# A new order of the work for a polysketch attention and MetaFormer kernel, with epsilon added on GpSimd

## The chip, the core and the metric

The kernel runs on one core of one Trainium2 chip. A core has TensorE (matrix multiply, PE in the profile), VectorE (DVE), ScalarE (ACT), GpSimd (POOL) and SyncE (SP, which here only issues transfers). The metric is device time in microseconds; what is compared is the median of several runs.

## What is computed

Inputs are q, k, v of shape (4 batches, 4 heads, 1088 rows, 32), two sketch matrices S1, S2 of 8 x 32, a scale g of 128 and two MLP matrices of 128 x 512 and 512 x 128. The weights arrive in 64-bit floats. The reference, cut to what matters:

```python
def phi(x):                      # 8 x 8 = 64 features of a row
    a = np.einsum('rd,bhsd->bhsr', S1, x)
    b = np.einsum('rd,bhsd->bhsr', S2, x)
    return np.einsum('bhsi,bhsj->bhsij', a, b).reshape(*x.shape[:-1], r * r)
q_p, k_p = phi(q), phi(k)
kv = np.einsum('bhsf,bhsd->bhfd', k_p, v)
z = np.sum(k_p, axis=2)
num = np.einsum('bhsf,bhfd->bhsd', q_p, kv)
den = np.einsum('bhsf,bhf->bhs', q_p, z)[..., None] + 1e-06
x = (num / den)                  # then (B, H, S, D) -> (B, S, 128)
xn = (x - mean(x)) / np.sqrt(var(x) + 1e-06) * g
out = x + np.maximum(xn @ w_ch1, 0.0) @ w_ch2
```

## The kernel before

All work is a flat list of small named operations, the string `PROGRAM` (L824 to L909), written out in the source; a loop at L910 calls them one after the other. Each operation issues one or a few instructions to one engine, so the string fixes the order on every engine: every engine runs its own instructions strictly in the order of the list and waits at an instruction until what it reads is ready and what it overwrites is free. The tile framework (`manual_schedule`, L65) only puts in the semaphores. SyncE's transfers are also issued in the order of the list, and a transfer that must wait holds up those behind it. The first argument of many operations says the engine (V VectorE, A ScalarE, G GpSimd, S SyncE); numbers behind it are batch or chunk, a range of row groups, and the banks of PSUM (`ALL`, eight banks of 512 columns).

Each batch of 1088 rows is two chunks of 512 rows and 64 rows left over. Chunks 0 to 7 belong two by two to batches 0 to 3; chunks 8 and 9 collect the 64-row rests of two batches each. Row groups u of 128 rows are counted 0 to 8: 0 to 4 is the first chunk of a batch, 4 to 9 the second with the rest.

What a batch goes through:

- Loads: `ld` (k, and q of batches 1 to 3), `ld_t` and `ld_tr` (q of batch 0, by heads and halves), `ld_v` and `ld_vr` (v by groups), all on SyncE's queue. `ld_s` (S1, S2) is on ScalarE's queue, `ld_g` on GpSimd's, `ld_w` brings the two halves of w1 (256 KB each) and w2 (512 KB).
- Weights: `w_ex`, `w_bits`, `w_exf`, `w_mant`, `w_low`, `w_e2`, `w_e3`, `w_add` or `w_addlow`, and `w_mul` turn the words of the 64-bit floats into 32-bit floats (index 0: S, 1: w1, 2: w2). `s_heads` writes S for all heads (tile `s_f`); `sk`, `sk_0`, `sk_8`, `sk_2`, `sk_d` spread it into the forms that the matmuls read. `fold` and `fold_cp` multiply the centring and g into w1.
- k features: `turn_g`, `turn_r` transpose k on VectorE (L414, L424); batch 0 multiplies with `k_dir` (L448) and copies with `k_cp`, the others use `k_feat` (L466) and `k_tok` (L475). `k_prod0` and `k_prod` make the 64 products (tile `kp`, one buffer), `k_sum`, `k_zs`, `k_sc`, `k_sccp` the sum z, `k_val` (L519) the product with v, `k_vcp`, `k_spr`, `k_rcp` bring it into the form `kvr`.
- q features: batch 0 turns q on TensorE (`turn_p`, `turn_c`) and uses `q_dir` (L554) and `q_cp`; the others use `q_feat` (L587) and `q_tok` (L596). `q_ac`, `q_den`, `q_rec` make 1/den, `q_a2` scales by it, `q_prod` makes the 64 products, `q_turn` (L634) transposes them.
- `num` (L648) is the numerator, 32 matmuls of 32 x 32 tiles for one range of rows. `num_cp` and `num_r` copy it, transposed, to `xT`, from which the MLP reads. `row_turn` (L710) makes rows of it, `row_wr` and `row_rd` pass them through DRAM.
- MLP: `hid` (L757) is one quarter of the hidden layer of a chunk (512 columns at most), `relu` (L765, L767) empties it, `sec` (L773) is the second matrix for 128 rows. The normalisation's scale comes from `st_bn`, `st_ag` and `st_pow` (statistics, variance plus epsilon, power -0.5: tiles `st`, `mv`, `va`, `rstd`) and is put on afterwards by `fin`, or by `fin_a` and `fin_g`, which also add x. `store` and `store_r` write the output.
- `fill` (L247) multiplies ones at the start, with no use of the result.

In the list before, batch 0 does its numerators in the order `num 0 0 4`, `num 0 4 9`, and the MLP begins with chunk 0 in eight half-wide `hid` of 256 columns. `st_ag` adds epsilon on VectorE (L737), `st_pow` raises to the power on GpSimd (L743).

Of the kernel before, what the change touches and what calls it, by code (L numbers as in the profile page):

```python
# [25 lines left out]
def kernel(  # L26
# [705 lines left out]
    @op  # L732
    def st_ag(c):
        n, st, mv = tiles(c), sts[slot(c)], mvs[slot(c)]
        for t in range(n):
# [1 line left out]
        dve.tensor_tensor(out=vas[slot(c)][:, 0:n], in0=_ap(mv, 0, P, 1, [[2, n]]),  # L737
                          in1=eps[:, 0:n], op=ALU.add)
# [116 lines left out]
    row_turn 1 1 2 3; w_low A 2 0 512; hid 5 0 3 2 4; q_den 1 4 9; ld_v S 1 0; hid 3 0 0 2 4;
    ld_vr S 1 1; w_exf V 2 0 512; ld_v S 2 0; turn_g k 3 0 4; turn_r k 3; relu A 0 0 1 0 2;
    ld_v S 2 2; ld_vr S 2 1; relu A 4 1 3 0 4; row_turn 1 0 6 7; q_a2 G 1 0 4; num_r A 0 6 7;
    q_prod G 1 0 4; hid 0 0 1 2 4; hid 4 0 2 2 4; relu A 0 0 1 2 4; row_wr S 1; q_rec 1 4 9;
    k_feat 3 6 7; turn_r q 2; relu A 1 0 3 0 2; ld_v S 3 2; hid 0 1 2 0 4; ld_v S 2 3;
    row_wr S 0; q_a2 G 1 4 9; q_prod G 1 4 9; w_e2 G 2 0 512; turn_g q 2 0 4; relu A 4 0 2 2 4;  # L860
# [83 lines left out]
```

## Time and profile before

| what | value |
|---|---|
| median of 3 runs | 113.13 us (111.95 to 113.26) |
| span of the profiled execution, first to last instruction | 111.1 us; the page gives no other time of this execution |
| busy: TensorE, VectorE, ScalarE, GpSimd | 98.5, 82.4, 36.7, 52.9 us |
| mean granted clock of TensorE | 0.965 |
| HBM read, written | 9.84 MB, 4.33 MB |

The profile is one execution recorded by the hardware. Its page gives the busy time of each engine, the span in 40 slices (each digit the busy share in tenths, 9 for 90% and more; the clock row the clock that was granted), the transfers, the chain of work that ended last, and the costliest groups of instructions by line. Other views of the same trace are a timeline (start, length, engine, line, operation, output<-input, count, and in brackets the idle time before with what ended it), the list of waits (who waited for whom, total, times, longest), and a table of stretches. PEld is TensorE's loading of weights, which overlaps its matmuls; a 32-bit matmul appears as two weight loads and two matmuls. L87 and L82 are helper lines for products and copies, so there the tile names tell what is meant. What ends a wait is inferred from semaphores, and "issue" means that the profile shows nothing that was waited for.

### The profile page before, as it was taken

How to read it: one execution, taken by the hardware profiler on the slowest of the kernel's cores; microseconds unless marked ns; L12 is line 12 of the kernel's file. 1: busy time of each engine (PE TensorE's matmuls, PEld its weight loads, DVE VectorE, ACT ScalarE, POOL GpSimd, SP SyncE). 2: the span in 40 equal slices, each digit the busy share in tenths (PEclk: the TensorE clock that was granted, in tenths of full speed). 3: DMA queues.
4: the chain of work that ended last, by engine and by line, in shares of the span. 5: the costliest groups of instructions: out<-in, count | busy, mean ns of one | idle time of the engine just before them, and what ended most of it. 6: DMA issues, size and time to landing. Idle time of an engine off the chain costs nothing.

```text
span 111.1 us, 3153 instructions
## 1 busy us (share of the span) xinstructions
PE 98.5 (89%) x1271; PEld 69.7 (63%) x1271; DVE 82.4 (74%) x238; ACT 36.7 (33%) x91; POOL 52.9 (48%) x70
## 2 busy tenths in 40 slices
PE   4988997891499999999999997999999999999960
...
PEclk9999999999556999999999999999999999999998
...
GB/s 31 262 249 249 285 249 204 279 252 246 91 6 120 163 122 298 40 94 112 83 102 51 0 0 100 44 110 139 113 171 6 101 289 59 50 0 187 12 135 74
DMA packets 16992, 14.37 MB, mean 129 GB/s; under 512 B 6609, under 2 KB 13777, under 8 KB 16977
## 3 DMA queue, kind: packets, MB, share of 16 engines
...
q8 instruction: 10, 0.16, 0.7%
q10 hardware_dynamic: 112, 0.04, 0.1%
...
q0 software_dynamic: 32, 0.00, 0.0%
HBM read 9.84 MB, written 4.33 MB: 127 GB/s over the span
## 4 chain that ended last, share of the span: by engine, by line
PE 65%; DVE 18%; DMA 9%; SPq 3%; issue 2%; DVEq 0%
PE ALL L757 27%; PE ALL L773 25%; DMA kn<-in_k_dram 9%; PE ALL L648 6%; PE ALL L519 4%; DVE qpT L634 3%; DVE kT L414 2%; SPq L143 2%; DVE hT L767 2%; DVE va L737 2%; DVE bits L279 2%; DVE fq L596 1%; DVE kf L475 1%; PE ALL L504 1%; DVE st L730 1%
## 5 line engine op out<-in xcount | busy, mean ns | idle before, releaser
L773 PEld LDWEIGHTS ALL<-w,hT 128*128 128x128 f32 x272 | 32.2, 192 | 3.9 <-issue 2.3
L773 PE MATMUL ALL<-w,hT 128*128 128x128 f32 x272 | 33.3, 277 | 0.0
L757 PE MATMUL ALL<-xT,w 128*128 128x512 f32 (+1 forms) x72 | 32.4, 586 | 0.0
L765 ACT ACTIVATE hT<-ALL 128x512 f32<-128x512 f32 (+2 forms) x31 | 14.0, 493 | 23.5 <-PE ALL L757 22.6
L743 POOL TENSOR_TENSOR rstd<-va,mhalf 128x4 f32<-128x4 f32 (+1 forms) x10 | 9.2, 926 | 23.8 <-DVE va L737 15.1
L757 PEld LDWEIGHTS ALL<-xT,w 128*128 128x128 f32 x72 | 13.8, 210 | 9.5 <-issue 5.3
L87 POOL TENSOR_TENSOR kp<-kf 128x1280 f32<-128x1280 f32 (+2 forms) x7 | 14.4, 2069 | 0.0
L87 POOL TENSOR_TENSOR qp<-a,fq 128x512 f32<-128x512 f32 (+3 forms) x8 | 13.3, 1678 | 0.8 <-DVE a L87 0.6
L648 PE MATMUL ALL<-qpT,kvr 32*32 32x288 f32 (+2 forms) x320 | 8.1, 388 | 4.2 <-DVE rden L616 3.9
L634 DVE STREAM_TRANSPOSE qpT<-qp 128x1280 f32<-128x1280 f32 (+2 forms) x9 | 11.1, 1230 | 0.0
L791 ACT ACTIVATE ob<-ALL,rstd 128x128 f32<-128x128 f32 x20 | 6.3, 368 | 14.3 <-PE ALL L773 9.4
L767 DVE TENSOR_SCALAR hT<-ALL 128x512 f32<-128x512 f32 (+1 forms) x13 | 7.5, 589 | 4.5 <-PE ALL L757 4.4
L82 ACT COPY xT<-ALL 128x256 f32<-128x256 f32 x12 | 7.0, 658 | 9.8 <-PE ALL L648 9.8
L648 PEld LDWEIGHTS ALL<-qpT,kvr 32*32 32x32 f32 x320 | 4.6, 108 | 8.0 <-issue 3.6
L710 DVE STREAM_TRANSPOSE xh<-ALL 128x256 f32<-128x256 f32 x16 | 6.6, 426 | 2.8 <-ACT xT L82 1.8
L730 DVE BATCH_NORM_STATS2 st<-x 128x6 f32<-128x128 f32 x32 | 6.7, 270 | 2.2 <-DMA x<-xd 2.2
L247 PE MATMUL ALL<-ones 128*128 128x512 f32 (+1 forms) x14 | 6.9, 635 | 1.4 <-DVE ones L190 1.4
L414 DVE STREAM_TRANSPOSE kT<-kn 128x1024 f32<-128x1024 f32 (+1 forms) x5 | 5.1, 1022 | 1.8 <-DMA kn<-in_k_dram 1.8
L305 POOL TENSOR_SCALAR ex<-exf 128x256 uint32<-128x256 f32 (+1 forms) x2 | 3.1, 1535 | 7.0 <-DVE exf L287 6.9
L519 PEld LDWEIGHTS ALL<-kp,vn 128*32 128x32 f32 x288 | 4.3, 110 | 2.7 <-issue 2.3
L786 DVE SCALAR_TENSOR_TENSOR ob<-ALL,rstd,x 128x128 f32<-128x128 f32 x12 | 4.0, 346 | 2.6 <-PE ALL L773 2.6
L519 PE MATMUL ALL<-kp,vn 128*32 128x64 f32 x288 | 5.1, 220 | 0.9 <-issue 0.9
...
## 6 DMA issues: line engine op xcount, KB each, us to landing
vn<-in_v_dram SPq DMA_DIRECT2D x16, 128.0 KB, 5.3
...
```

The source lines that it names most:

```text
L82: act.copy(o, i)
L87: by[eng].tensor_tensor(out=o, in0=a, in1=b, op=ALU.mult)
L414: dve.transpose(_ap(dst[b % 2], 0, P, 32 * g0, [[32, g1 - g0], [P, 8], [1, 32]]), src[b][:, 256 * g0 : 256 * g1],)
L519: pe.matmul(bank(z, 0, F)[D * h : D * h + D], vn[b][:, TW * h + D * u : TW * h + D * (u + 1)], kp[:, H * F * u + F * h : H * F * u + F * ( ...
L634: dve.transpose(_ap(qpT, 0, P, 32 * u0, [[32, u1 - u0], [TW, 8], [1, 32]]), qp[:, H * F * u0 : H * F * u1])
L648: pe.matmul(bank(z[r], o, o + w)[D * h : D * h + D], kvr[b % 2][rows, DM * f + D * h : DM * f + D * h + D], qpT[rows, c : c + w], start=(f ...
L730: dve.bn_stats(out=sts[slot(c)][:, 6 * t : 6 * t + 6], in_=row_ap(c, t))
L743: pool.tensor_tensor(out=rstds[slot(c)][:, 0:n], in0=vas[slot(c)][:, 0:n], in1=mhalf[:, 0:n], op=ALU.pow)
L757: pe.matmul(bank(z, 0, n), w1[:, P * j : P * (j + 1)], cols(c)[:, a : a + n], start=True, stop=True)
L765: act.activation(o, i, AF.Relu)
L767: by[eng].tensor_scalar(out=o, in0=i, scalar1=0.0, scalar2=None, op0=ALU.max)
L773: pe.matmul(bank(z, DM * t, DM * (t + 1)), h[:, 512 * j + P * t : 512 * j + P * (t + 1)], w2[:, DM * j : DM * (j + 1)], start=(j == 0), st ...
```

## The change

`st_ag` no longer adds epsilon; `st_pow` adds it on GpSimd before the power. All else is the list: the same 522 operations, each once, in another order, some of them on another engine (of w2's conversion, `w_e2` and `w_exf` leave GpSimd and VectorE for VectorE and ScalarE, `w_mul` goes from VectorE to GpSimd) and with other PSUM banks. In batch 0 the second range of rows goes first: `q_dir`, `q_prod`, `q_turn` and `num` for 4 to 9 stand ahead of those for 0 to 4, and the MLP begins with chunk 1 in four `hid` of 512 columns; `num 0 0 4` follows behind these. The transfers have a new order too: one half of w1 and one of k 0 first, w2 and v 0 ahead of k 2 and q 1. Of the list, the start and the part around `num 2` to `num 3` are shown, old and then new.

```diff
@@ -734,12 +734,12 @@
         n, st, mv = tiles(c), sts[slot(c)], mvs[slot(c)]
         for t in range(n):
             dve.bn_aggr(out=mv[:, 2 * t : 2 * t + 2], in_=st[:, 6 * t : 6 * t + 6])
-        dve.tensor_tensor(out=vas[slot(c)][:, 0:n], in0=_ap(mv, 0, P, 1, [[2, n]]),
-                          in1=eps[:, 0:n], op=ALU.add)
 
     @op
     def st_pow(c):
         n = tiles(c)
+        pool.tensor_tensor(out=vas[slot(c)][:, 0:n], in0=_ap(mvs[slot(c)], 0, P, 1, [[2, n]]),
+                           in1=eps[:, 0:n], op=ALU.add)
         pool.tensor_tensor(out=rstds[slot(c)][:, 0:n], in0=vas[slot(c)][:, 0:n],
                            in1=mhalf[:, 0:n], op=ALU.pow)
 
@@ -822,90 +822,89 @@
@@ -822,90 +822,89 @@
     PROGRAM = """
-    c_iota; c_ones; ld_t S 0 4 8; ld_s A 1; ld_t S 0 0 4; ld_s A 0; fill 1 512 7; w_ex V 0 0 64;
-    w_exf V 0 0 64; c_pads 1; c_masks; fill 1 256 6; ld_w S 1 0 2; fill 1 512 7; w_low A 1 0 256;
-    w_bits V 1 0 256; ld S k 0 16 34; c_ident; c_small; c_vpad 0; w_bits V 0 0 64;
-    w_ex V 1 0 256; w_mant V 0 0 64; ld_t S 1 4 8; ld_t S 1 0 4; w_e2 V 0 0 64; ld S k 0 0 16;
-    ld_w S 1 2 4; fill 1 512 6; turn_r k 0; w_e3 V 0 0 64; ld_tr S; w_exf A 1 0 256; c_vpad 3;
-    w_addlow V 0 0 64; s_heads V; ld_t S 2 4 8; turn_g k 0 0 2; w_mant A 1 0 256; c_ac 0; sk 7;
-    fill 1 512 6; sk_0 7; ld_t S 2 0 4; fill 1 256 5; turn_g k 0 2 4; k_dir 0 0 3 6; sk_2 7;
-    c_pads 0; ld S k 1 0 34; w_ex V 1 256 512; ld_t S 3 0 4; k_dir 0 6 9 5; w_add V 1 0 256;
-    k_dir 0 3 6 4; w_bits V 1 256 512; sk_8 7; w_exf V 1 256 512; w_mant V 1 256 512; c_vpad 2;
-    ld_t S 3 4 8; k_cp A 0 0 3 6; sk_q 7; ld S k 2 0 34; ld_g; turn_p 3 8 9; w_e2 V 1 0 256;
-    w_low A 1 256 512; fill 1 256 2; k_cp A 0 6 9 5; ld_v S 0 1; k_cp A 0 3 6 4; sk_d 7;
-    w_e3 V 1 0 256; k_sum 0 5; turn_p 2 0 4; turn_c A 2 0 4; w_e2 G 1 256 512; ld_v S 0 0;
-    k_prod0 0 3 6 0; w_add V 1 256 512; turn_r k 1; w_e3 V 1 256 512; ld S q 1 0 34; ld_vr S 0 0;
-    ld_v S 0 2; ld_v S 0 3; k_zs 0 5; k_sc 0 5; k_prod0 3 6 4 3; turn_p 6 4 8; k_sccp A 0 5;
-    turn_g k 1 0 4; q_dir 0 4 2; ld_vr S 0 1; turn_c A 3 8 9; turn_g k 2 0 4; turn_c A 6 4 8;
-    w_mul G 1 256 512; q_dir 4 9 6; k_prod G 0 6 9; q_cp A 0 4 2 0 24; q_ac G 0 0 4;
-    k_feat 1 2 3; q_cp A 4 9 6 0 24; w_mul G 1 0 256; q_den 0 0 4; c_cg G; turn_r k 2;
-    q_rec 0 0 4; q_ac V 0 4 9; c_ac 1; q_a2 V 0 0 4; q_den 0 4 9; k_tok 1 2 3; q_rec 0 4 9;
-    fold 4 0 256; q_prod G 0 2 4; c_rest; q_a2 V 0 4 9; k_feat 2 5 6; k_tok 2 5 6;
-    q_prod G 0 0 2; q_prod G 0 6 9; k_sum 1 7; q_prod G 0 4 6; turn_r q 1; sk_qq 2; k_sum 2 3;
-    k_zs 1 7; turn_g q 1 0 4; k_sc 1 7; fold 6 256 512; fold_cp A 6 256 512; k_sccp V 1 7;
-    q_turn 0 2; k_zs 2 3; k_val 0 0 3 5; q_turn 2 4; k_val 0 3 6 5; c_vpad 1; k_val 0 6 9 5;
-    k_sc 2 3; ld_v S 1 2; ld_v S 1 3; k_vcp A 0 5; ld_w S 2 0 4; k_spr 0 5; k_rcp A 0 5;
-    k_sccp V 2 3; ld S k 3 0 34; ld_vr S 1 0; q_turn 4 9; q_feat 1 6 7 2 3; q_tok 1 0 6 7;
-    q_tok 1 1 2 3; ld_v S 3 3; fold_cp A 4 0 256; w_bits V 2 0 512; num 0 0 4 0 1 4 5;
-    num_cp A 0 0 0 4 0 1; num_cp A 0 1 0 4 4 5; num 0 4 9 6 7 2 3; k_prod G 1 0 5; q_ac V 1 4 9;
-    q_ac V 1 0 4; row_turn 0 0 0 1; hid 0 0 0 0 2; ld_v S 2 1; w_ex V 2 0 512;
...
-    fin_a 6 2 3; fin_g V 0; q_feat 3 0 1 6 7; q_tok 3 0 0 1; q_tok 3 1 6 7; fin_a 2 1 2;
-    k_prod G 3 0 5; q_ac G 3 4 9; fin_a 3 2 0; num 2 0 9 2 3 4 5; num_cp A 2 0 0 4 2 3;
-    store S 0 0 4; k_val 3 0 9 0; num_cp A 2 0 4 8 2 3; q_ac G 3 0 4; row_turn 5 1 4 5;
-    num_cp V 2 1 4 8 4 5; row_turn 4 1 4 5; hid 7 8 3 0 1; relu A 7 8 3 0 1; k_vcp V 3 0;
...
+    ld_w S 1 2 4; ld_s A 0; c_pads 1; c_small; c_ones; ld_g; c_act; ld S k 0 0 16; ld_s A 1;
+    fill 1 256 1; ld_w S 1 0 2; c_ac 0; c_vpad 1; c_vpad 0; ld_tr S; c_iota; c_ident;
+    fill 1 256 3; c_masks; ld_t S 3 4 8; c_vpad 3; fill 1 512 7; c_pads 0; ld S k 0 16 34; c_rest;
+    w_ex V 1 256 512; w_ex V 0 0 64; w_exf V 1 256 512; ld_t S 1 4 8; w_e2 V 1 256 512;
+    w_bits V 1 256 512; ld_t S 0 4 8; w_bits V 0 0 64; fill 1 512 2; w_exf V 0 0 64;
+    w_e2 V 0 0 64; ld_t S 2 4 8; w_mant V 0 0 64; w_e3 V 0 0 64; w_addlow V 0 0 64; ld S k 1 0 34;
+    s_heads V; w_low A 1 0 256; w_ex V 1 0 256; ld_w S 2 0 4; turn_p 5 8 9; w_mant V 1 256 512;
+    w_low A 1 256 512; sk 4; w_bits V 1 0 256; ld_t S 3 0 4; w_exf A 1 0 256; w_mant V 1 0 256;
+    turn_g k 0 0 2; w_add G 1 256 512; ld_vr S 0 0; fill 1 512 2; sk_0 4; c_cg G; ld_t S 0 0 4;
+    turn_r k 0; turn_g k 0 2 4; ld_v S 0 1; sk_8 4; w_e2 V 1 0 256; k_dir 0 0 3 0; ld_v S 0 0;
+    w_e3 V 1 256 512; w_e3 V 1 0 256; ld_vr S 0 1; k_dir 0 3 6 6; k_cp A 0 0 3 0;
+    w_mul G 1 256 512; sk_q 4; k_prod0 0 3 0 0; fill 1 256 1; k_cp A 0 3 6 6; c_ac 1;
+    w_add G 1 0 256; k_dir 0 6 9 1; sk_2 4; k_prod0 3 6 6 3; w_mul G 1 0 256; turn_p 3 4 8;
+    k_cp A 0 6 9 1; ld_v S 0 3; turn_c A 5 8 9; k_sum 0 7; sk_d 4; k_prod G 0 6 9; turn_c A 3 4 8;
+    k_zs 0 7; turn_g k 1 0 4; k_sc 0 7; fold 3 0 256; k_sccp A 0 7; q_dir 4 9 2;
+    fold_cp A 3 0 256; turn_r k 1; ld_v S 0 2; w_low A 2 0 512; w_bits V 2 0 512; w_ex V 2 0 512;
+    ld_t S 2 0 4; k_feat 1 4 5; q_cp A 4 9 2 0 24; ld_t S 1 0 4; fill 1 512 1; w_exf A 2 0 512;
+    k_tok 1 4 5; q_ac G 0 4 9; ld S k 2 0 34; w_mant A 2 0 512; c_vpad 2; q_den 0 4 9;
+    ld S q 1 0 34; k_sum 1 7; q_rec 0 4 9; fold 3 256 512; w_e2 V 2 0 512; ld_v S 1 1;
+    q_a2 V 0 4 9; ld_v S 1 2; w_e3 V 2 0 512; k_val 0 0 3 6; q_prod V 0 6 9; q_prod G 0 4 6;
+    k_val 0 3 6 6; k_val 0 6 9 6; turn_p 2 0 4; k_zs 1 7; k_vcp A 0 6; k_prod G 1 0 5; q_turn 4 9;
+    k_sc 1 7; turn_c A 2 0 4; k_spr 0 6; fold_cp A 3 256 512; q_dir 0 4 1; k_rcp A 0 6;
+    k_sccp V 1 7; turn_g k 2 0 4; num 0 4 9 4 5 2 3; q_cp A 0 4 1 0 24; q_ac G 0 0 4; turn_r k 2;
+    w_add G 2 0 512; q_den 0 0 4; k_feat 2 6 7; num_cp A 0 1 4 8 2 3; num_cp V 0 0 4 8 4 5;
+    q_rec 0 0 4; hid 1 1 3 0 4; q_a2 G 0 0 4; row_turn 1 0 4 5; row_turn 1 1 2 3; q_prod G 0 2 4;
+    k_tok 2 6 7; row_wr S 1; num_r A 0 4 5; hid 0 1 1 0 4; relu A 1 1 3 0 4; ld S q 2 0 34;
+    turn_r q 1; turn_g q 1 0 4; q_prod G 0 0 2; ld_vr S 1 0; hid 7 1 2 0 4; relu A 0 1 1 0 4;
+    k_sum 2 6; q_turn 2 4; w_mul G 2 0 512; relu A 7 1 2 0 4; row_rd S 1; q_feat 1 3 4 0 1;
+    ld_v S 1 0; k_zs 2 6; q_turn 0 2; hid 7 1 0 0 4; ld_v S 1 3; k_prod G 1 5 9; q_tok 1 0 3 4;
...
+    sec 7 3 2; relu A 5 8 2 0 1; q_tok 3 1 0 1; sec 6 2 3; q_ac G 3 0 4; hid 3 8 3 0 1;
+    relu A 6 8 0 0 1; num 2 0 9 4 5 1 2; q_ac G 3 4 9; fin_a 7 3 2; q_den 3 0 4; relu A 3 8 3 0 1;
+    st_bn 8; k_prod G 3 0 5; st_ag 8; hid 3 8 1 0 1; num_cp A 2 0 4 8 4 5; sec 7 3 0;
+    relu V 3 8 1 0 1; num_cp A 2 0 0 4 4 5; num_cp V 2 1 4 8 1 2; sec 0 2 1; row_turn 5 0 4 5;
+    num_cp A 2 1 0 4 1 2; st_pow 8; fin_a 7 3 3; row_turn 5 1 1 2; sec 3 8 0; num_r A 2 4 5;
+    fin_a 7 3 0; q_den 3 4 9; row_wr S 5; fin_a 0 2 1; q_rec 3 0 4; q_rec 3 4 9; row_turn 4 0 4 5;
+    q_a2 G 3 0 4; hid 7 4 2 0 4; k_prod V 3 5 9; sec 5 3 1; row_turn 4 1 1 2; hid 0 4 0 0 4;
+    q_a2 V 3 4 9; row_wr S 4; relu A 7 4 2 0 4; q_prod V 3 0 4; ld_v S 3 0; fin_a 3 2 2;
+    hid 4 4 1 0 4; fin_a 6 2 3; fin_g G 2; q_turn 0 4; hid 1 5 2 0 4; hid 7 5 0 0 4;
+    q_prod V 3 4 9; relu A 1 5 2 0 4; relu A 4 4 1 0 4; k_val 3 0 9 5; fin 3 8 0; q_turn 4 9;
+    hid 4 5 1 0 4; fin_a 5 3 1; k_vcp A 3 5; store_r S 8 0; row_rd S 4; relu A 7 5 0 0 4;
+    k_spr 3 5; row_rd S 5; hid 3 4 3 0 4; k_rcp A 3 5; relu A 4 5 1 0 4; num 3 0 9 6 7 1 2;
+    relu A 0 4 0 0 4; relu V 3 4 3 0 4; hid 3 5 3 0 4; row_turn 7 0 6 7; row_turn 6 1 1 2;
...
```

More of the change, by code (lines that the diff above doesn't have):

```diff
@@ L855 @@
[L855 to L860, printed above, removed]
@@ L861 @@
-    row_rd S 0; relu A 5 0 3 2 4; ld_vr S 2 0; relu A 3 0 0 2 4; k_tok 3 6 7; k_val 1 0 9 3;
-    k_vcp A 1 3; k_sum 3 7; q_feat 2 5 6 1 2; q_turn 0 4; k_zs 3 7; k_spr 1 3; k_sc 3 7;
-    q_turn 4 9; relu A 0 1 2 0 4; q_tok 2 0 5 6; hid 0 1 0 0 4; k_rcp A 1 3; w_add G 2 0 512;
-    k_sccp V 3 7; ld_v S 3 0; w_e3 V 2 0 512; hid 3 1 1 0 4; num 1 0 9 6 7 4 5; w_mul V 2 0 512;
-    relu A 3 1 1 0 4; q_tok 2 1 1 2; ld S q 3 0 34; relu A 0 1 0 0 4; sec 3 1 1; num_r V 1 4 5;
-    row_pe 8 2; row_rd S 1; num_cp A 1 0 4 8 6 7; k_prod G 2 0 5; sec 1 0 1; row_cp A 8 2;
```

82 lines of the change are left out of this document (41 added, 41 removed).

## The prediction

> **What bounds it now.** I read first the page's busy times and its forty slices, then the table of stretches, then the chain that ended last, the timelines, and the list of waits.
>
> ```profile
> span 111.1 us, 3153 instructions
> PE 98.5 (89%) x1271; PEld 69.7 (63%) x1271; DVE 82.4 (74%) x238; ACT 36.7 (33%) x91; POOL 52.9 (48%) x70
> PE   4988997891499999999999997999999999999960
> PEclk9999999999556999999999999999999999999998
> GB/s 31 262 249 249 285 249 204 279 252 246 91 6 120 163 122 298 40 94 112 83 102 51 0 0 100 44 110 139 113 171 6 101 289 59 50 0 187 12 135 74
> ```
>
> TensorE is full in nearly every slice from the twelfth on; before that its work is small and waits for VectorE; in slice 10 (25.0 to 27.8 us) it stops, and in slices 11 to 13 its clock is down. The stretches give this its numbers (columns: busy time and instructions of PE, PEld, DVE, ACT, POOL, granted clock, DMA share, GB/s):
>
> ```profile
> 25.70:29.43 3.73, 0.00 (x0) 0.10 (x1) 3.56 (x8) 0.25 (x1) 1.56 (x2) 0.84 0.85 194
> 30.96:35.00 4.04, 4.04 (x14) 3.19 (x10) 3.93 (x10) 2.17 (x6) 1.40 (x3) 0.50 0.01 3
> 35.00:107.44 72.44, 71.26 (x868) 51.46 (x866) 53.92 (x158) 25.18 (x65) 32.76 (x28) 1.00 0.32 103
> 96.41 3.57 PE ALL L773 x32
> 76.20 6.11 PE ALL L757 x14
> ```
>
> So the run has three parts: a start until the first MLP matmul (`hid`, L757) at 30.96; 76.48 us in which TensorE has no room (30.96 to 107.44); and 3.66 us of last `fin` and stores (to 111.1). The second part holds 4.04 us at half clock, worth 2.02 us. Only the start, that half clock and a few stops can be shortened: the matmuls are the same ones. The last two rows are the chain's, and give their pace: a `sec` tile is eight matmuls of 0.111 (0.89), a 512-wide `hid` two of 0.436 (0.87).
>
> **The stop at 25.7.** The list of waits puts it down to VectorE's reciprocal:
>
> ```profile
> PE ALL L648 <- DVE rden L616: 3.9, 1, 3.9
> 29.43 1.03 PEld L648 LDWEIGHTS ALL<-qpT,kvr 32*32 32x32 f32 x47 [3.63 <-issue]
> 0.00:25.71 25.71, 21.64 (x347) 14.12 (x348) 20.63 (x63) 8.61 (x21) 15.71 (x39) 1.00 0.92 229
> 25.71:68.50 42.79, 38.82 (x634) 27.29 (x634) 34.64 (x92) 16.58 (x42) 28.28 (x23) 0.92 0.35 101
> 69.55 0.11 PEld L519 LDWEIGHTS ALL<-kp,vn 128*32 128x32 f32 x1 [1.05 <-issue]
> q8 instruction: 10, 0.16, 0.7%
> q8 instruction: 1, 0.02, 5.9%
> ```
>
> I don't believe it: `num 0 4 9` reads no reciprocal of batch 1, and is under way when it stops. [...] The last row is the DMA list of 26.8 to 28.2 us: one such packet; the list of 20.1 to 26.8 has none. So I read both stops as code pages that came late, the first because the load queue was full until about 28 us.
>
> [...]
>
> [...] In the trace the second stop came where `num 2` and `k_val 3` follow each other (65.93 to 69.55, 3.6 us); the new order has no such pair. I price code pages at 0, with 0 to 1.5 us as bounds.
>
> **The new start, step by step.** Rows for it (start, length):
>
> ```profile
> 1.69 1.28 ACT L301 ACT_TABLE_LOAD   x1 [1.69 <-PEq L928]
> 2.98 0.18 DVE L274 TENSOR_SCALAR ex<-s_raw 8x64 uint32<-8x64 uint32 x1 [1.60 <-DMA s_raw<-in_S_dram]
> 6.03 0.41 DVE L87 TENSOR_TENSOR s_f<-mant,bits 8x256 f32<-8x256 f32 x1
> 9.42 2.08 PEld L448 LDWEIGHTS ALL<-sk,kT 128*128 128x128 f32 x18 [0.93 <-DVE kT L414]
> 14.14 2.25 PE L554 MATMUL ALL<-skd,qT 128*128 128x96 f32 x18
> 17.43 0.70 PE L352 MATMUL ALL<-w1g,cg 128*128 128x256 f32 x2 [0.40 <-POOL cg L347]
> 16.42 0.56 ACT L82 COPY fq<-ALL 128x480 f32<-128x480 f32 x1 [0.64 <-PE ALL L554]
> 47.45 0.52 POOL L87 TENSOR_TENSOR ac<-fq 128x160 f32<-128x160 f32 x1
> 17.84 1.07 POOL L87 TENSOR_TENSOR qp<-a,fq 128x512 f32<-128x512 f32 x1 [0.35 <-DVE a L87]
> 17.68 0.32 DVE L609 TENSOR_REDUCE den<-ac 128x20 f32<-128x180 f32 x1
> 18.62 0.23 DVE L616 RECIPROCAL rden<-den 128x20 f32<-128x20 f32 x1
> 32.08 0.41 DVE L287 TENSOR_SCALAR exf<-ex 128x512 f32<-128x512 uint32 x1
> 42.90 0.67 DVE L310 SCALAR_TENSOR_TENSOR bits<-w_raw,ex 128x512 uint32<-128x512 uint32 x1
> 13.21 0.94 DVE L87 TENSOR_TENSOR kp<-ALL,kf 128x768 f32<-128x768 f32 x1
> 22.82 1.50 DVE L634 STREAM_TRANSPOSE qpT<-qp 128x1280 f32<-128x1280 f32 x1
> 14.07 1.23 DVE L414 STREAM_TRANSPOSE kT<-kn 128x1024 f32<-128x1024 f32 x1
> 31.07 0.61 DVE L84 COPY xT<-ALL 128x256 f32<-128x256 f32 x1 [1.80 <-PE ALL L648]
> 23.73 1.82 PE L648 MATMUL ALL<-qpT,kvr 32*32 32x128 f32 x80
> ```
>
> *Loads.* Ahead of the last piece of v 0 stand now 3,776 KB, then 3,072 KB (k 2 and q 1 go behind). At about 250 GB/s (the GB/s row) from 2 us on that is 14 us, plus a landing of 1 to 2 us: before its use near 19. [...]
>
> *Sketch.* `ld_s A 1` now stands behind `c_act` and its table load: issued near 3.0 instead of 1.4, S there near 5.0 instead of 2.98. Behind it VectorE has seven small steps of about 0.15 (half of them overlap, so less than the 0.18 of the row), three w1 steps of 0.28 and `s_f` 0.41, to 7.3; four more w1 steps of 0.28, to 8.4; both halves of `turn_g k 0` with `sk_0` and `turn_r` between (0.7 + 0.2 + 0.2 + 0.7): `k_dir` at 10.3 instead of 9.42. Bounds: 9.4, if S comes as early as now, to 11.
>
> *To the first numerator.* `k_dir` to `q_dir` took 14.14 - 9.42 = 4.7 us; now half a fold (0.6) goes between, so `q_dir 4 9` starts at 15.6 and ends 10 x 0.112 later, at 16.7. Then copy 0.56, `q_ac` on GpSimd 0.52, `q_den` 0.32, `q_rec` 0.23, `w_e2` 0.41, `q_a2` 0.33 (as `q_den`), `w_e3` 0.67, `q_prod V` 0.94, `k_zs` 0.15, `q_turn` 1.50 = 5.63, and five hand-offs between engines, an estimate of 0.1 each: 22.9. `w_e3` and `q_prod V` read two SBUF operands while GpSimd does its own `q_prod` (1.07), and one such wait I add (next rows): 24.0. Behind `q_turn` VectorE does `k_sccp` 0.2, `turn_g k 2` 1.23, `turn_r` 0.2, `q_den` 0.26, `num_cp` 0.61: 26.5, and **the first `hid` starts at 26.6** instead of 30.96. Bounds: 24.1, with `k_dir` at 9.4 and neither wait nor hand-offs; 28.5, with a `k_prod` of 1.94 (row below) in between too.
>
> ```profile
> 53.67 1.20 DVE L737 TENSOR_TENSOR va<-mv,eps 128x1 f32<-128x1 f32 x1
> 52.92 1.94 POOL L87 TENSOR_TENSOR kp<-kf 128x1024 f32<-128x1024 f32 x1
> 62.54 1.82 DVE L737 TENSOR_TENSOR va<-mv,eps 128x4 f32<-128x4 f32 x1
> vn<-in_v_dram SPq DMA_DIRECT2D x16, 128.0 KB, 5.3
> L737 DVE TENSOR_TENSOR va<-mv,eps x10: 159/164/1822, 49.4 to 97.9; 128x4 f32<-128x4 f32 x8, 128x1 f32<-128x1 f32 x2
> ```
>
> An addition whose median is 0.16 us took 1.20 and ended just after GpSimd's product, at 54.86; the 1.82 has a product beside it in the same way: VectorE waited them out. This is what moving epsilon removes: 1.0 + 1.7 us of VectorE. TensorE had other matmuls, and lost at most the gap of about half a microsecond before `num 2` at 65.93; I count 0. The ten additions cost GpSimd about 0.3 us each (between VectorE's 0.16 and `q_ac`'s 0.52), 3 us of an engine that is 48% busy, and lengthen the last rstd by 0.1 to 0.4, hidden by the last `hid` and `sec`. The bank pairs are neighbours in the old list too (0 1, 6 7, 2 3, 4 5): 0.
>
> **The full part.** Its 76.48 us lose the half clock, 2.02, and the stop at 69.55, 0.9. Moved from the start into it are `q_feat 1` 0.54 (23.19 to 23.73), `num 0 0 4` 1.31 (23.73 to 25.04), `k_sum 2` 0.31 and `k_sc 2` 0.31: 2.47. That is 76.0. New in it: `ld_v S 3 0` is issued only behind `row_wr S 4`. From `num 2` to `k_val 3` TensorE has 8.1 us; VectorE reaches `row_turn 4 1` after 4.6, the queue issues the load at about 5.1, and it lands up to 5.3 later (the median of v, most of them in the crowded start): at 10.4 at the latest. I take 0.5, with 0 to 2.3. `row_wr S 1` waits for `row_turn 1` near 27 and holds q 2 and half of v 1 behind it; v 1 is needed by `k_val 1` near 36, 5.3 of landing end near 33: hidden. `store_r S 8 0` stands ahead of `row_rd S 4` and 5, but its `fin` is done by then, 0. `w_mul` of w2 goes to GpSimd (1.07, as its `q_prod` of 128x512), behind both `q_prod` of chunk 0, and ends near 30.5; the first `sec` comes near 32: hidden by the four `hid` of chunk 1 (3.5); without that cover, rival 3. The end keeps its shape: 3.66.
>
> **Sum:** 26.6 + 76.0 + 0.5 + 3.7 = 106.8 us of span against 111.1. The page has no time of its own beside the span; the median of the runs is 2.0 above it (the lowest 0.9), so I add 2.0: **108.8 us**.
>
> **Rivals.** *1. Nothing waits in the start:* first `hid` at 24.1 and no v stall: 103.8, so 105.8 us. For it: the waits are estimates. Against: eight VectorE steps in a row have no slack.
> *2. The stop comes back,* VectorE's or a page's: 3.73 and the 2.02 of half clock after it on top, 112.5, so 114.5 us (+1.2%). For it: the list of waits, and loads are still dense at 18 us. [...]
> *3. GpSimd blocks VectorE (the slower case).* Place: 19 to 37 us, where `w_e3`, `q_prod V 0`, `q_ac V 1` and `q_a2 V 1` stand beside GpSimd's longer list. If each waits out one product of 1.94, that is 7.8, 6.7 more than counted; TensorE then idles as long as at 25.7, and 2.02 of half clock follow: 115.5, so 117.5 us. It loses to the old kernel from 4.3 us on the path. Against: in the old trace only two of ten `va` were caught.
> [...]
> *4. The change does not do what it says:* epsilon and bank pairs alone give 0, and if the order only shifts waits, 113.
>
> **Chances.** Forecast 0.55 (own range 106.8 to 110.8), rival 1 0.11, rival 2 0.14, rival 3 0.12, rival 4 0.08. A measurement can tell 2% here, 110.9 to 115.4. Faster: 0.66; within: 0.22; slower: 0.12. The range takes in rival 2 and most of rival 1: 105.5 to 114.6.
>
> **What would show it.** Right: first L757 matmul at 25 to 28.5; no stop above 1 us of "issue" in L648 or L519; granted clock 1.0 from 28 to 36; last L773 about 103; every `va` now POOL's. Wrong: `k_dir` after 11; a stop of 3 us and a 5 in the clock row; L765, L767 or L773 waits for POOL-made tiles; a stop at `k_val 3` over 2.3 us.

## The result, and the profile after

The changed kernel takes 105.72 us (median of four runs, 105.54 to 105.9) where the kernel before takes 112.99 (median of four, 111.95 to 113.26): a ratio of 0.937, 95% interval 0.930 to 0.944. Medians are over all runs of a kernel, while ratios, here and in the table below, leave out runs more than 1.5% above the kernel's fastest. The forecast was 108.8 in a range of 105.5 to 114.6. The profiled execution took 105.89 us, and its span is 104.1, so 1.8 lie around the span.

The page of the changed kernel, its lines for the engines, the clock and the transfers:

```profile
span 104.1 us, 3156 instructions
PE 96.4 (93%) x1271; PEld 68.3 (66%) x1271; DVE 77.0 (74%) x222; ACT 39.6 (38%) x96; POOL 54.4 (52%) x81
PE   4996989799999999999999999999999999999950
PEclk9999999999999999999999999999999999999999
GB/s 76 267 228 350 205 165 375 128 5 58 288 198 4 117 202 178 268 127 245 206 186 0 6 0 0 101 151 6 154 70 272 238 111 201 0 107 0 101 39 87
```

The hole in TensorE's row and the dip in the clock row are gone, and the load queue falls silent at about 21 us (5 GB/s in the ninth slice). The stretches, cut as in the prediction at the first MLP matmul and behind the last second-layer one (columns as there):

```profile
0.00:24.27 24.27, 20.30 (x280) 13.42 (x280) 20.19 (x58) 10.15 (x23) 14.80 (x37) 1.00 0.73 194
24.27:100.44 76.17, 76.05 (x992) 54.89 (x992) 56.46 (x164) 29.45 (x73) 39.63 (x45) 1.00 0.40 124
100.44:104.07 3.63, 0.00 (x0) 0.00 (x0) 0.35 (x1) 0.00 (x0) 0.00 (x0) 1.00 0.21 72
```

So the three parts are 24.27 + 76.17 + 3.63, where 26.6 + 76.5 + 3.7 was forecast. Two of three terms were right to 0.4 us; the start was 2.3 us shorter than forecast. It reads, from the timelines of the engines:

```profile
1.38 1.28 ACT L199 ACT_TABLE_LOAD   x1 [1.38 <-PEq L927]
1.45 0.29 ACTq L112 DMA_DIRECT2D s_raw<-in_S_dram  x1
9.70 1.55 PE L448 MATMUL ALL<-sk,kT 128*128 128x64 f32 x12 [1.00 <-DVE kT L414]
14.16 1.28 PE L554 MATMUL ALL<-skd,qT 128*128 128x96 f32 x10
18.00 0.69 DVE L310 SCALAR_TENSOR_TENSOR bits<-w_raw,ex 128x512 uint32<-128x512 uint32 x1
18.60 1.83 DVE L87 TENSOR_TENSOR qp<-a,fq 128x768 f32<-128x768 f32 x1
22.19 1.33 PE L648 MATMUL ALL<-qpT,kvr 32*32 32x160 f32 x64
24.27 2.83 PE L757 MATMUL ALL<-xT,w 128*128 128x512 f32 x6
```

The steps keep the order of the forecast. What is to be seen besides: the second load of S is issued at 1.45, inside the table load, and not behind it; and `q_prod V` takes 1.83 us, 0.89 more than the 0.94 of the same width before, so it did wait out one GpSimd product, as forecast (`qp`, 18.23 to 19.62, stands beside it), while `w_e3` (0.69) did not.

### The profile page after: what moved, and what is told of

Its sections match the earlier page's. It is cut to its first block, busy times and chain, and to the rows that moved or that the text cites. A ratio compares the mean times of both kernels' runs of the same rounds, so it can differ in the third digit from the quotient of the medians.

```text
span 104.1 us, 3156 instructions
## 1 busy us (share of the span) xinstructions
PE 96.4 (93%) x1271; PEld 68.3 (66%) x1271; DVE 77.0 (74%) x222; ACT 39.6 (38%) x96; POOL 54.4 (52%) x81
## 4 chain that ended last, share of the span: by engine, by line
PE 65%; DVE 20%; DMA 7%; issue 2%; ACT 2%; POOL 2%; POOLq 0%; DVEq 0%; ACTq 0%
PE ALL L757 27%; PE ALL L773 23%; PE ALL L648 4%; DMA xd<-xh 4%; DMA x<-xd 3%; PE ALL L519 2%; PE ALL L554 2%; DVE kp L87 2%; DVE qp L87 2%; DVE st L730 2%; PE ALL L587 1%; DVE xh L710 1%; PE ALL L466 1%; ACT xT L82 1%; DVE kT L414 1%
## 5 line engine op out<-in xcount | busy, mean ns | idle before, releaser
L765 ACT ACTIVATE hT<-ALL 128x512 f32<-128x512 f32 (+2 forms) x35 | 16.7, 500 | 22.7 <-PE ALL L757 17.0
L757 PEld LDWEIGHTS ALL<-xT,w 128*128 128x128 f32 x72 | 12.1, 190 | 7.6 <-issue 5.2
L87 POOL TENSOR_TENSOR qp<-a,fq 128x512 f32<-128x512 f32 (+2 forms) x7 | 12.2, 1745 | 3.1 <-DVE a L87 2.9
L87 POOL TENSOR_TENSOR kp<-kf 128x1280 f32<-128x1280 f32 (+2 forms) x6 | 13.2, 2211 | 0.0
L741 POOL TENSOR_TENSOR va<-mv,eps 128x4 f32<-128x4 f32 (+1 forms) x10 | 2.1, 206 | 17.1 <-DVE mv L736 17.1
L767 DVE TENSOR_SCALAR hT<-ALL 128x512 f32<-128x512 f32 (+2 forms) x9 | 5.1, 571 | 5.6 <-PE ALL L757 5.6
L247 PE MATMUL ALL<-ones 128*128 128x512 f32 (+1 forms) x14 | 7.7, 688 | 1.5 <-DVE ones L190 1.5
L801 POOL TENSOR_TENSOR ob<-ob,x 128x512 f32<-128x512 f32 x3 | 3.9, 1296 | 5.4 <-ACT ob L791 5.4
L596 DVE STREAM_TRANSPOSE fq<-ALL 128x576 f32<-128x576 f32 x6 | 4.5, 768 | 1.6 <-PE ALL L587 1.6
L247 PEld LDWEIGHTS ALL<-ones 128*128 128x128 f32 x14 | 3.4, 268 | 3.4 <-issue 1.5
L87 POOL TENSOR_TENSOR ac<-fq 128x160 f32<-128x160 f32 (+1 forms) x6 | 3.1, 528 | 4.6 <-DVE fq L596 2.7
```

Source lines behind the costliest of these rows:

```text
L87: by[eng].tensor_tensor(out=o, in0=a, in1=b, op=ALU.mult)
L247: pe.matmul(bank(z, 0, w), ones[:, 0:P], ones[:, 0:w], start=True, stop=True)
L757: pe.matmul(bank(z, 0, n), w1[:, P * j : P * (j + 1)], cols(c)[:, a : a + n], start=True, stop=True)
L765: act.activation(o, i, AF.Relu)
```

## Theories, and what each makes of the time

A page is here one packet of queue q8, whose kind the profile calls "instruction" (10 packets, 0.16 MB in the kernel before). *Page theory* (the prediction's): the old kernel loses 3.7 us to a code page of TensorE that comes late, 2.0 to the half clock behind it and 0.9 to a second page; the new order merely has no such moment. *VectorE theory*: the stop is the wait for a reciprocal that the list of waits names. *Order theory*: chunk 1 ahead of chunk 0 is itself the gain. *Epsilon theory*: VectorE's lost time at epsilon is real time. Later came the *port theory* (a name only, no run shows a port): once the stop is gone, VectorE waiting out GpSimd's products, above all while w2 is decoded, is what is late next. All ratios are to the kernel before, on the same chip:

| run | us, median | ratio (95% interval) |
|---|---|---|
| changed kernel | 105.72 | 0.937 (0.930 to 0.944) |
| before, epsilon on GpSimd | 111.66 | 0.988 (0.981 to 0.996) |
| before, loads later | 116.66 | 1.027 (1.017 to 1.037) |
| before, gate in the load queue | 113.13 | 1.004 (0.998 to 1.011) |
| before, gate and epsilon | 111.85 | 0.996 (0.989 to 1.004) |
| before, gate, epsilon, w2 out of the way | 109.0 | 0.959 (0.951 to 0.968) |
| changed, epsilon back on VectorE | 107.8 | 0.952 (0.945 to 0.958) |
| changed, chunk 0 first | 105.61 | 0.941 (0.938 to 0.945) |
| changed, w2 late | 116.38 | 1.032 (1.025 to 1.039) |
| changed, loads crowded | 110.7 | 0.986 (0.980 to 0.992) |
| changed, product of chunk 1 on VectorE | 110.33 | 0.980 (0.971 to 0.990) |
| the same, one more filler | 105.27 | 0.941 (0.938 to 0.944) |

## Experiments on the stop

**More fillers.** Each `fill 1 512 z` of the old kernel becomes `fill 5 96 z`, each `fill 1 256 z` becomes `fill 3 64 z`; nothing else.

```
-    fill 1 512 7
+    fill 5 96 7
-    fill 1 256 6
+    fill 3 64 6
...
```

> The kernel before, in which the seven filler matmuls of the start become 29 narrower ones of about the same total length, 88 instructions of TensorE more. [...] VectorE theory: the first numerator runs through, and the stop is 11 instructions into the second one as before, 783 instructions from the start.

By the page theory the stop comes again behind 695 matmuls and weight loads, now inside the first numerator, and the kernel takes 111 to 114 us. One run took 119.28 us, outside these: the narrow fillers were slower than I had counted, and the sketch's first matmul came at 14.25 instead of 9.42. So the time says nothing, but the place does. A stretch, from the start to the stop:

```profile
0.00:33.29 33.29, 30.53 (x347) 27.26 (x348) 19.61 (x61) 7.79 (x19) 14.44 (x38) 1.00 0.80 200
```

and TensorE's timeline on both sides of the stop:

```profile
32.67 0.89 PE L648 MATMUL ALL<-qpT,kvr 32*32 32x128 f32 x36
33.98 1.71 PE L648 MATMUL ALL<-qpT,kvr 32*32 32x128 f32 x92 [0.42 <-issue]
```

The stop stands again behind 347 + 348 = 695 instructions, 7.6 us later in time and now inside the first numerator (the 128-wide shape); TensorE goes on at 33.98, 4 us before VectorE computes the reciprocal in question (38.00). It is short, and the load queue was quiet by then (36 GB/s from 31 to 34 us). It has kept its count of 695 and left its place in the work, as the page theory has it; the VectorE theory is dead.

**Loads later.** In the old kernel, q of batch 2 and four pieces of v go behind the row writes.

```
-    ld_v S 3 3; ... ld_v S 2 1; ... ld S q 2 0 34; ... ld_v S 2 0; ... ld_v S 2 2; ld_vr S 2 1; ...
-    row_wr S 1; ...
+    row_wr S 1; ld S q 2 0 34; ld_v S 2 1; ld_v S 2 0; ld_v S 2 2; ld_vr S 2 1; ...
     row_rd S 0; ...
+    ld_v S 3 3; ...
```

> The kernel before, in which q of batch 2 and four pieces of v (1,072 KB, 4.3 us of the load queue at 250 GB/s) are issued behind the first row writes instead of ahead of them; no engine's order of computing is touched, and no instruction of TensorE. [...] VectorE theory (the wait for the reciprocal of batch 1): the stop stays at 3.7 us, 112.5 to 113.5 us. Order theory (chunk 1 first is what gains): 112 to 113.5 us.

By the page theory the page comes sooner, the stop shrinks to under 0.8 us, the half clock goes with it, and the time is 107 to 108.5 us. The stop did so, if not as fully (1.2 us are left), and the time did the opposite: 116.66 us. TensorE's and VectorE's timelines:

```profile
26.93 1.03 PE L648 MATMUL ALL<-qpT,kvr 32*32 32x160 f32 x48 [1.18 <-issue]
40.65 0.53 PE L490 MATMUL ALL<-kf 128*32 128x32 f32 x18 [3.57 <-DVE kf L475]
38.56 0.25 DVE L424 STREAM_TRANSPOSE qT<-qn 128x64 f32<-128x64 f32 x1 [4.54 <-DMA qn<-in_q_dram]
```

the queues' list of the transfers from 24.5 to 25.7 us:

```profile
q8 instruction: 1, 0.02, 5.8%
```

and a stretch:

```profile
40.40:47.30 6.90, 6.65 (x86) 2.92 (x91) 5.53 (x9) 0.80 (x2) 3.53 (x3) 0.51 0.58 176
```

The page came in that window instead of at 26.8 to 28.2, the stop at 695 shrank from 3.7 to 1.2 us, and the clock stayed full from 27 to 37 us. But the row writes were issued only at 33.9, q of batch 2 behind them, and VectorE stood 4.54 us for it; TensorE then paused 3.57 us and had the half clock again, from 40.4 to 47.3. So the half clock began at a long pause here too (3.57 us; in the kernel before at 28.2, in the pause from 25.7 to 29.4), and my edit had made this pause.

**A gate in the load queue.** To hold the loads back without that: a 256-byte transfer that reads batch 0's spread K'V, in the queue behind k of batch 3.

```
+    gd = dram.tile([1, 64], F32, name="gd")
+    @op
+    def gate(eng):
+        by[eng].dma_start(out=gd, in_=kvr[0][0:1, 0:64])
...
-    ld S k 3 0 34; ld_vr S 1 0;
+    ld S k 3 0 34; gate S; ld_vr S 1 0;
```

> The kernel before, with one tiny transfer (256 bytes of batch 0's spread K'V, to a scratch of its own) in the load queue behind k of batch 3, so that the queue sends the 1,360 KB behind it only from about 23.6 us on; the order of the loads and of every computing engine is as before. In the run with later loads the stop shrank to 1.0 us, but VectorE then waited 4.5 us for q of batch 2, which here comes by 29 us. [...] Order theory (only chunk 1 first brings the gain): 111.5 to 113.5 us.

By the page theory: a stop under 0.4 us, no half clock from 28 to 36, 107 to 108.5 us. Measured: 113.13 us, a ratio of 1.004. The 107 to 108.5 are refuted, though the stop in the second numerator is gone (0.45 us left, and that for VectorE). TensorE's, VectorE's and GpSimd's timelines:

```profile
27.54 1.03 PE L648 MATMUL ALL<-qpT,kvr 32*32 32x160 f32 x48 [0.45 <-DVE fq L596]
43.75 1.46 PE L779 MATMUL ALL<-w,hT 128*128 128x128 f32 x8 [2.08 <-DVE w L87]
40.91 2.69 DVE L87 TENSOR_TENSOR w<-mant,bits 128x512 f32<-128x512 f32 x1
40.21 2.83 POOL L87 TENSOR_TENSOR kp<-kf 128x1280 f32<-128x1280 f32 x1
```

and a stretch behind them:

```profile
44.30:47.80 3.50, 3.50 (x20) 3.50 (x19) 1.62 (x7) 1.26 (x3) 2.83 (x3) 0.51 0.05 11
```

Read the four timeline rows backwards. The first second-layer matmul (L779 here) waits 2.08 us for w2. VectorE makes w2 in 2.69 us, against 0.69 for the same instruction in the run with later loads: it starts beside a GpSimd product and is done 0.56 us after that product ends at 43.04; by these times it waited the product out. Two more losses stand beside it: a pause of 1.2 us in K'V of batch 0, up to 23.44, for which the profile names no cause ("issue"), and, behind the wait for w2, 3.5 us at half clock. So the stop had hidden other losses of about its own size: taken away alone, by this gate, it is worth nothing.

## Experiments on the rest

**Epsilon alone, and epsilon back.** The two lines of `st_ag` and `st_pow`, moved in the old kernel, and moved back in the changed one.

```
-        dve.tensor_tensor(out=vas[slot(c)][:, 0:n], in0=_ap(mv, 0, P, 1, [[2, n]]),
+        pool.tensor_tensor(out=vas[slot(c)][:, 0:n], in0=_ap(mvs[slot(c)], 0, P, 1, [[2, n]]),
                           in1=eps[:, 0:n], op=ALU.add)
```

> The kernel before, with epsilon added on GpSimd and nothing else changed. Page theory (nearly all of the gain is the stop at 25.7 us and the half clock behind it): the stop stays, 112.5 to 113.5 us. Epsilon theory (VectorE waiting out GpSimd's products costs real time): 110 to 111.5 us, by the 1.0 + 1.7 us that two of the ten additions lost.

> The changed kernel, with epsilon back on VectorE. Page theory: 105.5 to 106.2 us, no more than 0.4 above the changed kernel, though one or two of the ten additions may again take over 1 us. Epsilon theory: 107 to 108.5 us.

Measured: 111.66 and 107.8 us. Neither theory's numbers hold for the first (it lies between them); the second is the epsilon theory's. TensorE's timelines, two rows of the kernel before and two with epsilon on GpSimd:

```profile
30.96 6.57 PE L757 MATMUL ALL<-xT,w 128*128 128x256 f32 x18
45.04 1.16 PE L773 MATMUL ALL<-w,hT 128*128 128x128 f32 x8
31.07 5.85 PE L757 MATMUL ALL<-xT,w 128*128 128x256 f32 x18
44.59 1.13 PE L773 MATMUL ALL<-w,hT 128*128 128x128 f32 x8
```

These two executions differ by 1.2 us of span, and 0.45 of it is there at the first second-layer matmul, ahead of the first addition of epsilon (49.4 us in the old kernel): the half clock behind the stop lasted from 30.3 to 33.7 us, in the old kernel from 28.2 to 35.0. Behind the additions come 0.5 us at `num 2`, which now starts without its gap, and 0.2 at the stop in `k_val 3`. So by the traces about 0.7 us is epsilon's, where the medians say 1.5.

The profiled run of the second kernel had its clock halved from 10 to 20 us, which the other runs of it did not have, so only what comes later in it is read. Its additions as a group:

```profile
L737 DVE TENSOR_TENSOR va<-mv,eps x10: 159/161/2049, 37.0 to 97.6; 128x4 f32<-128x4 f32 x8, 128x1 f32<-128x1 f32 x2
```

VectorE's, GpSimd's and TensorE's timelines in it:

```profile
37.03 1.50 DVE L737 TENSOR_TENSOR va<-mv,eps 128x4 f32<-128x4 f32 x1
36.56 1.95 POOL L87 TENSOR_TENSOR qp<-a,fq 128x1024 f32<-128x1024 f32 x1
38.95 1.13 PE L757 MATMUL ALL<-xT,w 128*128 128x256 f32 x4 [0.82 <-DVE xh L710]
```

and the group of additions in the changed kernel:

```profile
L741 POOL TENSOR_TENSOR va<-mv,eps x10: 191/200/282, 34.0 to 91.8; 128x4 f32<-128x4 f32 x8, 128x1 f32<-128x1 f32 x2
```

Two of the ten additions are caught. The one at 37 us takes 1.50, behind a product of 1.95 us; the next row turn is late, and TensorE waits 0.82 for it. Against the changed kernel TensorE loses 1.1 us there and 0.6 more later: 0.4 at 72 us, 4 us behind the other caught addition (2.05 at 68.2), and 0.2 elsewhere; that these 0.6 come from epsilon is not shown. On GpSimd the ten additions take 0.2 us each. Epsilon's place is worth 1.1 to 1.7 (by the trace), 1.6 (by the ratios) or 2.1 us (by the medians) in the new order.

**Gate and epsilon.** The gated kernel with the epsilon edit in it.

> The kernel before with that gate in the load queue and epsilon on GpSimd, but none of the new order. If page, half clock and epsilon are the whole gain: 105.5 to 107 us, within 1.5% of the changed kernel. If the new order brings some 3 us of its own: 109 us or more.

Measured: 111.85 us. The number of the last case came, though for the reason that the gate alone had shown: TensorE waits for w2 here too (1.66 us). It pauses once more, ahead of the first MLP matmul. VectorE's and TensorE's timelines:

```profile
25.72 1.88 DVE L279 TENSOR_SCALAR bits<-w_raw 128x512 uint32<-128x512 uint32 x1
28.54 6.05 PE L763 MATMUL ALL<-xT,w 128*128 128x256 f32 x18 [1.65 <-DVE xh L710]
43.83 1.13 PE L779 MATMUL ALL<-w,hT 128*128 128x128 f32 x8 [1.66 <-DVE w L87]
```

VectorE's first step on w2 (L279) stands beside GpSimd's products (23.04 to 27.32) and takes 1.88 us, 0.38 in the run with the gate alone; the row turn behind it is late, TensorE waits 1.65 us for it, and its clock is halved from 28.2 to 31.6.

**Chunk 0 first.** In the changed list the chunks 0 and 1 of batch 0 change roles.

```
-    q_dir 4 9 2; ... num 0 4 9 4 5 2 3; ... hid 1 1 3 0 4; ... num 0 0 4 4 5 2 3; ...
+    q_dir 0 4 2; ... num 0 0 4 4 5 2 3; ... hid 1 0 3 0 4; ... num 0 4 9 4 5 2 3; ...
```

> The changed kernel with the roles of chunks 0 and 1 of batch 0 exchanged all through its list (loads of q, numerators, MLP, statistics): chunk 0 first again, everything else as in the new order. If which chunk goes first is worth nothing by itself: 105 to 106.5 us. If chunk 1 first is what gains: 108 us or more.

105.61 us: the same as the changed kernel. Which chunk comes first is worth nothing; the order theory, as its name has it, is dead. What the order does around it remained.

**w2 out of the way, in the old order.** On top of gate and epsilon:

```
-    w_exf V 2 0 512; ... w_e2 G 2 0 512; ... w_add G 2 0 512; ... w_e3 V 2 0 512; ... w_mul V 2 0 512;
+    row_turn 0 0 0 1; row_turn 0 1 4 5; w_bits V 2 0 512; ... q_den 1 0 4; w_exf A 2 0 512;
+    w_e2 V 2 0 512; w_e3 V 2 0 512; q_rec 1 0 4; ... q_prod G 1 0 4; w_add G 2 0 512; ...
+    q_prod G 1 4 9; w_mul G 2 0 512; ...
```

> The kernel before with the gate in the load queue and epsilon on GpSimd, and now the decoding of w2 taken out of GpSimd's way: its exponent on ScalarE, its two next steps on VectorE ahead of GpSimd's second product of batch 1 instead of beside it, its sum and its product on GpSimd between the products; both row turns of chunk 0 stand ahead of the first w2 step. New theory (port theory: without the stop, what is next late is VectorE waiting out GpSimd's products in w2's steps, 1.5 + 1.6 + 0.3 + 2.0 us in the gated kernel, and the first second-layer matmul waits for w2): the first MLP matmul comes 1.2 to 1.7 us earlier, the wait for w2 of 1.7 us is gone, 108.3 to 110.2 us against 111.85. If VectorE's waits are not what bounds it: 111.3 to 112.3.

In this run w2's mantissa is made from words that the step before has already overwritten, so w2 has other values; the instructions and their sizes are those of the description. 109.0 us, 2.9 less than with the gate and epsilon alone, inside the port theory's range; the runs spread from 107.67 to 111.08. TensorE's timeline:

```profile
27.04 1.56 PE L763 MATMUL ALL<-xT,w 128*128 128x256 f32 x6
29.66 0.70 PE L763 MATMUL ALL<-xT,w 128*128 128x256 f32 x2 [1.06 <-ACT hT L771]
31.22 4.54 PE L763 MATMUL ALL<-xT,w 128*128 128x512 f32 x10 [0.85 <-DVE xT L84]
43.27 1.16 PE L779 MATMUL ALL<-w,hT 128*128 128x128 f32 x8
```

The first MLP matmul is 1.5 us earlier than in the gated run with epsilon (28.54), and the first second-layer matmul follows the numerator without a wait. But only 0.6 us of this is left at that matmul (43.27 against 43.83): in between TensorE pauses 1.06 and 0.85 us, and its clock is halved from 31.9 to 35.3. This execution took 109.76 us, 1.3 less than the profiled one with the gate and epsilon. The two fastest runs, 107.67 and 108.25, had a granted clock of 0.999 and 1.0, so they were without that half clock.

**w2 late, in the new order.** The reverse: in the changed kernel only the steps of w2 go back among GpSimd's products.

```
-    w_bits V 2 0 512; w_ex V 2 0 512; ... w_exf A 2 0 512; ... w_e2 V 2 0 512; ... w_e3 V 2 0 512;
-    ... w_add G 2 0 512; ... w_mul G 2 0 512;
+    k_sccp V 1 7; w_bits V 2 0 512; w_ex V 2 0 512; ... row_turn 1 1 2 3; w_exf V 2 0 512; ...
+    q_prod G 0 0 2; w_e2 G 2 0 512; ... w_add G 2 0 512; ... k_sccp V 2 6; w_e3 V 2 0 512; w_mul V 2 0 512;
```

> The changed kernel with only the decoding of w2 put back where the kernel before has it: beside GpSimd's products of batch 0 and 1, the exponent and the last product on VectorE. Chunk 1 stays first, the page comes in time. Port theory: w2 is ready at 32 to 33 us instead of 28.2, the first second-layer matmuls wait 2 to 3 us, 107.5 to 109.5 us. If only the page and the first numerator matter: 105.5 to 106.3.

116.38 us, more than either said. Two losses stand beside each other. TensorE's and VectorE's timelines:

```profile
39.44 4.55 PE L773 MATMUL ALL<-w,hT 128*128 128x128 f32 x24 [2.98 <-DVE w L87]
37.06 2.24 DVE L87 TENSOR_TENSOR w<-mant,bits 128x512 f32<-128x512 f32 x1
```

and two stretches:

```profile
9.60:23.30 13.70, 13.20 (x85) 9.78 (x88) 6.52 (x17) 2.85 (x9) 4.46 (x7) 0.50 0.79 196
40.30:43.80 3.50, 3.50 (x19) 3.50 (x18) 3.40 (x16) 0.00 (x0) 2.80 (x4) 0.51 0.00 0
```

The first is the forecast one: TensorE waits 2.98 us for w2 and pays 3.5 us of half clock behind the pause; it is 5.3 us behind the changed kernel at the end of the first numerator and 10.8 at the end of these matmuls, so this loss is 5.5. The second, the 5.3 before it, comes with 13.7 us of half clock in the start, and no theory had expected it.

**Loads crowded, product on VectorE, one more filler.** Edits on the changed kernel; the third on top of the second.

```
-    ld_v S 1 2; ...
+    ld_v S 1 2; ld_vr S 1 0; ld_v S 1 0; ld_v S 1 3; ld_vr S 1 1; ld S q 2 0 34; ld S k 3 0 34; ld_v S 2 3; ld_v S 2 0; ...
```

> The changed kernel with 1.6 MB of loads (q of batch 2, k of batch 3, four pieces of v) issued ahead of the first row write instead of behind it, at 16 to 22 us, as the kernel before has it. [...]

```
-    q_prod V 0 6 9; q_prod G 0 4 6;
+    q_prod V 0 4 9;
```

> The changed kernel with the whole product of chunk 1 of batch 0 on VectorE (1,280 wide: an estimate of 1.57 us, 5/3 of 0.94) instead of 768 of it on VectorE (1.83, of which 0.9 waiting out GpSimd) and 512 on GpSimd (1.39). Port theory: the first numerator 0.2 to 0.3 us earlier, 105.2 to 105.8 us. If GpSimd's share was a real help: 106 or more.

```
-    fill 1 512 2; sk_0 4;
+    fill 1 512 2; fill 1 512 2; sk_0 4;
```

> The kernel of the run before (the changed kernel with the whole product of chunk 1 on VectorE, 110.33 us, its clock halved from 10.4 to 20.7 us) with one more filler matmul of 512 (0.86 us) behind the sketch's transposes, in the 0.73 us in which TensorE stands still at 9 us. If that pause is what halves the clock: no half clock in the start, 105.2 to 106.2 us, which would be the changed kernel's time or a little under it. If the half clock hangs on something else (the run, the chip, where the windows of the clock begin): 109.8 to 111 us as in the run before.

The first two took 110.7 and 110.33 us, and both had the clock halved in the start. Two stretches of the second:

```profile
6.90:10.40 3.50, 2.77 (x16) 1.82 (x15) 3.46 (x12) 0.51 (x1) 1.11 (x2) 1.00 0.98 302
10.40:20.70 10.30, 10.02 (x70) 8.10 (x69) 4.63 (x10) 4.02 (x12) 4.28 (x6) 0.50 0.94 226
```

TensorE's timeline of it:

```profile
9.79 1.61 PE L448 MATMUL ALL<-sk,kT 128*128 128x64 f32 x9 [0.73 <-DVE kT L414]
```

and of the third:

```profile
7.66 1.98 PE L247 MATMUL ALL<-ones 128*128 128x512 f32 x4
9.78 1.44 PE L448 MATMUL ALL<-sk,kT 128*128 128x64 f32 x11
```

By the page theory the crowded loads bring a stop of 1 to 2.5 us in the first numerator, or one of up to 2 us at 695, and 107 to 110 us. The run is no test of that: its first numerator was 4.7 us late and stands where the queue was quiet again (16 to 19 GB/s from 25 to 28 us), and TensorE met no stop. In the second the half clock covers what the edit does; its time says nothing. With the filler the pause is gone, the clock is full, and six runs lie between 105.2 and 105.57; the first numerator starts 0.27 us earlier than in the changed kernel (21.92 against 22.19), as the port theory has it. Whether the filler brought the clock back stays open: in this run the fillers of the start also reached their full pace by 5.5 us, in the run before only near 7, which would fit stretches of the clock that began elsewhere (more on this in the last section). By its ratio, 0.941, it is the changed kernel's time and not better.

## Why the prediction was right, and where it was not

- *The number:* 105.72 lies in the stated range, but below the forecast's own 106.8 to 110.8; it is that of rival 1 (105.8), for whose sake the range reached so low. Rival 1's mechanism, that nothing waits in the start, holds in part only: the first `hid` comes at 24.27, close to its 24.1, but `q_prod V` did wait out a product (0.89 us), and other steps made up for it. That the number fell into the range is luck to that extent. Of the signs named, the stops, the clock and the `va` came as said; the first `hid` was earlier than 25 to 28.5, and the last second-layer matmul ended at 100.4 instead of 103.
- *The stop is a page's, and does not come back:* right. Its count of 695 held when its place moved, and it shrank from 3.7 to 1.2 us when the page came sooner (in 24.5 to 25.7 us instead of 26.8 to 28.2). The 0 for code pages, with its bounds of 0 to 1.5 us, was the author's estimate: no run shows what a page costs by itself; in the changed kernel none of TensorE's matmuls waits with "issue" as the reason.
- *What its end is worth (3.73 + 2.02, the sum's largest part):* right for this change, wrong as a price of its own. Without the stop the old order gains nothing, since w2 is late next. The prediction checked this cover for the new order ("w_mul of w2 goes to GpSimd ... hidden by the four `hid`": forecast 30.5 for w2 and 32 for the first `sec`, measured 28.2 and 30.23) but did not see how much of the gain hangs on it (ratio 0.996 with the gate and epsilon, 0.959 with w2 out of the way as well, 0.937 for the whole change): its rival 3 put VectorE's waits for GpSimd into the new kernel, and it is the old order, its stop removed, that loses by them (2.08 us of wait for w2 with the gate).
- *"The first hid starts at 26.6":* 2.3 us too late. `k_dir` was put at 10.3 behind a table load that the load of S did not wait for (9.70 measured: 0.6); `q_dir 4 9` came 4.46 us after it, where 4.7 and a half fold of 0.6 were counted (0.8); and the way from there to the first MLP matmul took 10.1 instead of 11.0, with the one wait for GpSimd in it that was counted (0.9). `k_dir` and the first `hid` came within their bounds, and all three steps erred to the same side.
- *Epsilon, "I count 0":* this step failed. The row in hand, 1.0 + 1.7 us of VectorE lost, was set aside because TensorE had other matmuls, and half a microsecond of TensorE was seen and dropped. The runs show 1.5 us by the medians (0.5 to 2.1 by the interval) in the old order, of which the traces put about 0.7 down to epsilon, the dropped half microsecond among it; in the new order 1.1 to 2.1.
- *The stall of 0.5 at `k_val 3`:* did not come.
- *The full part, 76.0:* 76.17 measured, though epsilon's gain was left out of the sum. No waits took its place: TensorE stands idle for 0.12 us of it. It is busy for 76.05, where the prediction's rows give 75.75 (4.04 + 71.26, less 2.02, plus 2.47); which matmuls took the 0.3 more is open.
- *Bank pairs:* priced 0, not tried by themselves.

What remains between the old order without its stop, its epsilon and its late w2 (ratio 0.959) and the changed kernel (0.937) was not taken apart. In the trace of that run TensorE waits 1.06 us for ScalarE and 0.85 for VectorE between the first MLP matmuls; together these would be about the size of it, but that is argued, not shown. The half clock behind them is no part of it, since the two runs from which the 0.959 comes had none.
